# Q and K of one more token tile with tokens stationary, in a conditioned transformer block on one core

## The chip, the cores and the metric

The kernel runs on one core of one Trainium2 chip. The metric is the device time of one execution in microseconds, as the median of the runs shown. Engines are named as in the profile: PE (matrix products), DVE, ACT and POOL (vectors), SP (it issues nearly all transfers).

## The reference

One transformer block over 2048 tokens of 448 features, modulated by a vector `c`: dilated local attention (16 heads of 28, a window of 8 keys that are 2 tokens apart), then a GELU network of 1792 features. All in bfloat16.

```python
mod = (silu(c) @ w_mod).reshape(c.shape[0], 6, 1, -1)
sa, ca, ga, sb, cb, gb = ...
h = layernorm(x) * (1 + ca) + sa
# A: qkv = h @ wqkv; logits of token s against keys s, s-2, ..., s-14
#    attn = softmax(logits * 28 ** -0.5); o = attn @ v
x = x + ga * (o @ wo)
h = layernorm(x) * (1 + cb) + sb
# B: y = layernorm(h); gelu(y @ w1 + b1) @ w2 + b2
x = x + gb * B(h)
```

## The kernel before

**Tiles.** The tokens are dealt to two streams (even and odd), so that the dilated window becomes eight neighbouring tokens of one stream. Each stream has 1024 tokens, in 8 tiles of 128; a tile `p` of the code means 128 tokens of both streams. Attention goes in 9 batches of 114 queries of each stream.

**A tile's way.** `front_ln` takes the statistics (`stats`, `aggr`, `rstd`), normalizes into a buffer `zy` (`norm`, `tail`) and turns the features onto the partitions: tiles 0 and 1 by PE transposes (`tr0`, `tr1`), tiles 2 to 7 by DMA transposes on SP (`zT2` to `zT7`). The evacuation (`evac_h`, on ACT or DVE) applies scale and shift and writes `hT`. The scale and shift come from `mod_cols`, PE products of `w_mod` (buffers `wm_st`, `wm_r`, and `wm_d`, into which `twice` copies some columns on DVE), added up by `sca` on DVE.

**Q and K, in two ways.** `front_qk` keeps the weights stationary, which are first spread to 32 columns per head (`spread`, `spread r`); its result already has the features on the partitions, and one evacuation writes `qT` or `kT`. `natural_qk` keeps the tokens stationary (`hT` as weights, 448 columns of `wqk_st` moving): it needs no spread weights, but its result has the tokens on the partitions, so it is evacuated into a `zy` buffer and turned by a DMA transpose on SP (`tq`, `tk` with the tile's number, L631). The constant `NATURAL` says which tiles go the second way. Products of 64 rows (the last 64 of the 448 features) are issued apart from the full ones, as the `r` tasks beside the `f` tasks.

**Attention and the rest.** For batch i: V (`v`), scores (`lt`, two halves), exponential on ACT, mask on DVE, denominators (`pd`), weighted values (`po`), `omul` on DVE. Then for each tile `wo`, the first residual (`x1`), two layer norms and a DMA transpose (`yT`), and for two tiles at a time `w1`, GELU on ACT, `w2`, the last residual and the store. The products `mods` and a small round trip through memory give the other modulation rows.

**The order.** Nothing is scheduled at run time. The code records some 700 tasks with `add`, numbered in the order of recording, and `emit` issues them in the order of a list of numbers, `ORDER`; an entry `n:A`, `n:D`, `n:P` puts a task on ACT, DVE or POOL instead of its first engine, and `n:R` takes a V product with the rest first. An entry `n+18@m` issues 18 products of a zeroed tile (`filler`) ahead of task n, into the accumulator of task m. `SLOTS` gives each buffer its place; the products share four PSUM slots of two banks. Each engine runs its instructions in this order and waits where an operand or a slot isn't free. SP's transfers queue in its order too.

Of the kernel before, what the change touches and what calls it, by code (L numbers as in the profile page):

```python
# [14 lines left out]
S, D, H, DH, F = 2048, 448, 16, 28, 1792  # L15
# [17 lines left out]
EXP_SET = "natural_log_exp_and_others"  # L33
GELU_SET = "gelu_apprx_tanh_and_others"
UNITS = [[0], [1], [2, 3], [4, 5], [6, 7]]
NATURAL = range(2, 8)
PHASES = [(range(0, 5), [0]), (range(5, 7), [1]), (range(7, 9), [2, 3])]
ROOM = {"P": 4, "et": 2, "den": 2, "zy": 5, "h2": 3, "yT": 3, "hm": 2, "vb": 3, "xp": 3, "hw": 2}
SPLIT = 2
# [1 line left out]
ENGINE = {"A": "ACT", "D": "DVE", "P": "POOL", "R": "PE2"}  # L41
RATE = 310e3
SLOTS = [
# [6 lines left out]
]  # L50
ORDER = """
17 18 19 3 7 0 15 14 10 8 1 55+12@55 12 2 11 5 13 4 6 9 71 73 74 72 16 56 57 75 58 59 76 60 20 24 21 23 22 25 26 77 61
62 78 67 66 108 63+6@63 68 64 65 110 84:A 89:P 79 69 70 80 101 94 109 111 112:P 81 83 90 82 85:A 114 113 115:D 27 28
30 29 32 31 34 37 86:P 87 92:A 91:P 88:A 93:P 135 133 136 134 144 142 137 139 145 143 102 95 96 116 117:A 118:A 120:A
119:A 103 97 99 104 106 105 98 126 121 127 122 129 124 107 100 190 191 187 188 128 123 130 125 138 140:D 146 148 147
149:D 141 185 186 236:R 238 241 150 153:A 239 242 269 271 207 200 198 208 201 272 199 270 209 210 151 152 154 202 211
213 203 212 159 160 164 156 273 214 161 237 155 163 204 240 278 279 205:D 36 33 40 35 171 215 206 162 280 281 192 189
282:A 157 165 158 172 243 193 244 194 195 196 283 216 217 284 274 285:D 275 307:R 340 173 39 286 41 219 218 197 341:D
246 308 312 309 313 247 310 167 224 168 221 225 174 38 131 220 169 226 276:D 132 314 311 245 222 315 316 317 318 373
248 277 170 166 227 223 176 175 249 374 345 342 319 289:A 290:A 343 346 250 251 288:A 253 287 320 228 375 378 321  # L60
447:P 322 252 324 344 254 558:P 376 255 347 257 379 256 377 258 259 323 325 326 295 233 229 292 296 230 291 299 297
293 348 300 304 303 232 350 301 351 305 54 45 51 46 43 52 48 298 294 231 47 49 44 262 260 327 328 380 329 261 330 263
333 331 264 265 332 334 266 335 267 234 448 381 349 382 383 449 560 559 384 406 482:A 450 561 235 268 352 353 337 336
338 385 386 181 354 357 387 483 484 390 391 355 356 388 178 389 358 182 184 339 42 50 53 426 414 425 427 428 485 413
407 415 416 418 417 408 420 410 409 411 412 419 424 422 423 421 446 392 393 180 394 395 396 399 183 397 179 359 361
400 593:P 398 177 429 401 360 362 363 364 366 367 440 442 454 489 451 455 452 490 441 443 432 402 365 368 431 433 444
436 437 486 487 491 456 453 457 370 369 459 460 371:A 403 488 404 430 434 458 461 492 493 494 495 435 462 594 302 445
306 405 372 496 463 438 497 498 501 464 524 595 525 537 536 499 466 467 500 596:D 465 468 470 469 502 471 472 473 474
475 503 505 504 506 507 510 476 477 508 511 517 526 527 529 538 539 528 518 531 519 522 521 520 523 530 535 532 533
534 545 547 562 565 597 557 598 479 509 478 480:A 563 566 548 551 546 540 512 513 514 543 541 599 564 567 600 568 553  # L70
515:A 544 542 549 601 602 570 603 605 571 606 628 569 604 572 552 554 573 607 608 574 575 555 609 577 578 576 579 581
580 610 582 612 611 583 613 584 585 586 550 516 481 635 636 630 629 639 638 640 637 641 631 632 634 633 647 648 642
644 587 588 614 615 616 617 618 621 619 620 622 623 625 624 626:D 589 590 651 591 652 655 654 653 643 646 645 658 664
656 649 650 662 659 665 663 657 556 627 592 660 666 661 674 675 669 679 677 676 678 668 680 673 671 672 670 681 687
695 686 685 682 683 688 684 689 705 697 696 706 698 701 702 709 710 690 694 707 708 691 693 692 699 700 667 439 703
704 711 712
"""


# [74 lines left out]
def kernel(  # L154
# [18 lines left out]
    P = Plan()  # L173
# [336 lines left out]
    def front_ln(u, on_act, dma=False):  # L510
        np_ = len(u)
        if dma:
            zT = sb("yT", [128, NS * KT, 256], BF16, "zT")
        else:
            ptr = [psum("ptr", (128, np_, 2, NS, 128), BF16) for _ in range(2)]
        for q, p in enumerate(u):
            z = fixed("zy", zys)
            for n in range(NS):
                stats(lambda p=p, n=n: xn(p, n), 0, 2 * p + n, [f"x{p}"])
            rstd(0, 2 * p, 2, on_act)  # L520
            for n in range(NS):
                normalize(lambda z=z, n=n: z.t[:, n, 0:D], lambda p=p, n=n: xn(p, n), 0, 2 * p + n, [f"x{p}"],
                          bufs=[z], writes=[(z, n)])
            tail(z, [(z, 0), (z, 1)], (z, 2), p == 0)
            zk = [(z, 0), (z, 1), (z, 2)]
            if dma:
                add("SP", 2.0, lambda z=z, q=q: nc.sync.dma_start_transpose(
                    out=zT.t[:, :, 128 * q:128 * q + 128], in_=z.t[:].rearrange("p n e -> p (n e)")), reads=zk, bufs=[z, zT],
                    writes=[(zT, q)], xfer=1.0, name=f"zT{p}")
                continue  # L530

            def tr(q=q, z=z):
                for kt in range(KT):
                    for n in range(NS):
                        nc.tensor.transpose(out=ptr[kt % 2].t[:, q, kt // 2, n, :], in_=z.t[:, n, kt * 128:(kt + 1) * 128], identity=ident[:])
# [371 lines left out]
    for pi, (batches, tiles) in enumerate(PHASES):  # L907
# [55 lines left out]
```

## Time and profile before

| | |
|---|---|
| median of 3 runs | 171.34 us (170.38 to 173.87) |
| the profiled execution's own time | 169.54 us |
| its span, from the first to the last instruction | 167.7 us |
| PE, DVE, ACT, POOL busy | 96%, 69%, 63%, 27% of the span |
| mean granted TensorE clock | 0.999 |

The profile is of one execution. Busy shares are averages over the whole span; in a row of the timeline, the first number is the start in us from the span's start, the second the length, and the bracket at the end is the engine's idle time before it with what ended it. A `q` behind an engine's name is its queue, which issues transfers. Buffer numbers are left out of the names, and one line of code can stand for many tasks (L548 and L554 are the full and the 64-row products of every weight; L631 is every `tq` and `tk`).

### The profile page before, as it was taken

The numbers are of one execution on the slowest core, as the hardware profiler recorded it, in microseconds if no ns is written. First come the engines' busy times: TensorE is split into PE (matmuls) and PEld (weight loads), VectorE is DVE, ScalarE is ACT, GpSimd is POOL, SyncE is SP. The second block draws the span as 40 slices with busy tenths as digits, with TensorE's granted clock in tenths as the row PEclk, the third lists the DMA queues.
The fourth block names the chain that finished last, engine by engine and source line by source line (L and its number), as shares of the span: only waits on it lengthen the run. The fifth ranks groups of instructions, "written<-read, shape, count | busy, mean of one in ns | idle before, by whom it ended". The sixth has DMA issues, their size and how long they took to land.

```text
span 167.7 us, 4943 instructions
## 1 busy us (share of the span) xinstructions
PE 160.4 (96%) x2109; PEld 83.8 (50%) x2109; DVE 115.3 (69%) x268; ACT 105.2 (63%) x146; POOL 45.8 (27%) x72
## 2 busy tenths in 40 slices
PE   7779999999989999999999999999999999999993
PEld 4567655546444553445565444556534455444652
DVE  7798978937889989996567879893779650400032
ACT  3268799999878991869486086968428440086400
POOL 7063230000161301744340030850010347007200
PEclk9999999999999999999999999999999999999999
DMA  4998998999997998100075000009210005100024
GB/s 146 339 299 309 173 288 158 140 191 164 233 313 158 219 210 195 35 4 0 26 153 73 4 0 0 0 4 151 33 59 0 0 20 105 59 0 0 0 72 147
DMA packets 35573, 18.78 MB, mean 112 GB/s; under 512 B 28507, under 2 KB 34592, under 8 KB 35552
## 3 DMA queue, kind: packets, MB, share of 16 engines
q1 hardware_dynamic: 35548, 18.47, 48.7%
q8 instruction: 16, 0.26, 0.7%
q14 instruction: 5, 0.04, 0.1%
q10 hardware_dynamic: 4, 0.00, 0.0%
HBM read 9.81 MB, written 1.84 MB: 69 GB/s over the span
## 4 chain that ended last, share of the span: by engine, by line
PE 80%; DMA 7%; DVE 6%; ACT 4%; issue 1%; SPq 0%; DVEq 0%
PE p L883 26%; PE p L548 22%; PE pq L548 6%; PE pw L803 5%; PE p L554 4%; DMA kT<-zy 3%; PE po L771 3%; PE pv L548 3%; PE lt L738 2%; DMA b_rows<-in_B_b_dram 2%; DMA zT<-zy 2%; PE pq L562 2%; ACT et L745 2%; PE pq L554 2%; PE pd L760 1%; ACT vb L721 1%
## 5 line engine op out<-in xcount | busy, mean ns | idle before, releaser
L864 ACT ACTIVATE hm<-p,b_col 128x512 bf16<-128x512 f32 x56 | 33.9, 692 | 34.9 <-PE p L554 28.0
L883 PE MATMUL p<-w_s,hm 128*128 128x448 bf16 (+1 forms) x238 | 44.3, 342 | 0.0
L548 PE MATMUL p<-yT,w_s 128*128 128x512 bf16 x168 | 38.0, 379 | 0.0
L469 POOL TENSOR_TENSOR rs_all<-mvs,neg_half 128x2 f32<-128x2 f32 x22 | 16.4, 760 | 61.9 <-DVE mvs L458 61.8
L883 PEld LDWEIGHTS <-hm 128*128 128x128 bf16 x238 | 22.6, 98 | 19.5 <-issue 1.3
L889 DVE TENSOR_TENSOR x_all<-p,x1p 128x896 bf16<-128x896 f32 (+2 forms) x10 | 8.9, 900 | 26.6 <-PE p L883 26.6
L548 PEld LDWEIGHTS <-w_s 128*128 128x128 bf16 x168 | 16.0, 98 | 20.7 <-issue 2.5
L745 ACT ACTIVATE et<-lt 128x928 bf16<-128x928 f32 x18 | 16.2, 942 | 7.4 <-PE lt L738 7.3
L456 DVE BATCH_NORM_STATS2 stt<-x_all 128x6 f32<-128x448 bf16 x32 | 18.7, 612 | 0.3
L841 POOL TENSOR_TENSOR x1p<-x_all,gbb_bc 128x448 f32<-128x448 bf16 x16 | 17.2, 1099 | 0.0
L548 PE MATMUL pq<-wqk_st,hT 128*128 128x448 bf16 x72 | 15.0, 353 | 0.0
L788 DVE TENSOR_TENSOR qT<-po,den 128x912 bf16<-128x912 f32 x9 | 9.9, 1104 | 5.7 <-ACT den L782 4.9
L751 DVE TENSOR_TENSOR et<-et,mask 128x928 bf16<-128x928 bf16 x18 | 12.5, 724 | 1.7 <-ACT et L745 1.5
L803 PE MATMUL pw<-wo_s,qT 128*128 128x448 bf16 x64 | 13.1, 353 | 0.1
L819 DVE TENSOR_TENSOR h<-h,mod_bc 128x896 bf16<-128x896 bf16 x16 | 11.4, 710 | 0.3
L628 ACT CAST zy<-pq 128x896 bf16<-128x896 f32 x12 | 10.5, 907 | 0.5 <-issue 0.2
L810 DVE TENSOR_TENSOR x_all<-pw,x_all 128x896 bf16<-128x896 f32 x8 | 8.7, 1085 | 2.7 <-PE pw L803 2.7
L548 PEld LDWEIGHTS <-hT 128*128 128x128 bf16 x72 | 6.5, 98 | 6.4 <-issue 0.9
L782 ACT ACTIVATE den<-den,den_bias 128x928 f32<-128x928 f32 x9 | 9.5, 1066 | 0.2
L456 DVE BATCH_NORM_STATS2 stt<-h 128x6 f32<-128x448 bf16 x16 | 9.4, 611 | 0.2
L689 POOL COPY hw<-hT 128x1024 bf16<-128x1024 bf16 x3 | 3.3, 1114 | 22.7 <-ACT hT L504 22.7
L780 ACT ACTIVATE den<-pd 128x928 f32<-128x928 f32 x9 | 8.4, 939 | 1.1 <-PE pd L760 1.1
(114 smaller groups left out, 183.4 us busy)
## 6 DMA issues: line engine op xcount, KB each, us to landing
w_s<-in_B_w_dram SPq DMA_DIRECT2D x7, 224.0 KB, 3.4
out_dram<-x_all SPq DMA_DIRECT2D x7, 224.0 KB, 2.2
x_all<-in_A_x_dram SPq DMA_DIRECT2D x3, 448.0 KB, 4.6
wmod<-in_w_mod_dram SPq DMA_DIRECT2D x3, 448.0 KB
w_s<-in_B_w_dram SPq DMA_DIRECT2D x3, 448.0 KB, 4.7
wqk_st<-in_A_wqkv_dram SPq DMA_DIRECT2D x3, 225.0 KB
wm_st<-in_w_mod_dram SPq DMA_DIRECT2D x1, 672.0 KB
x_all<-in_A_x_dram SPq DMA_DIRECT2D x2, 224.0 KB
```

Of the source, the lines that this page charges most:

```text
L456: add("DVE", 0.53, lambda: nc.vector.bn_stats(out=stt[:, w, b, 0:6], in_=src()), reads=reads, bufs=bufs, after=early if w == b == 0 else ( ...
L469: ways = {"POOL": (0.55 + 0.17 * n, lambda: nc.gpsimd.tensor_tensor(out=r, in0=v, in1=neg_half[:, 0:n], op=ALU.pow))}
L548: nc.tensor.matmul(out(), lhsT=lhs(kt, slice(0, 128)), rhs=rhs(kt, slice(0, 128)), start=first and kt == 0, stop=not first and kt == KT - 2)
L554: nc.tensor.matmul(out(), lhsT=lhs(KT - 1, rows), rhs=rhs(KT - 1, rows), start=first, stop=not first, tile_position=(rows.start, 0))
L628: add("ACT", 0.80, lambda to=to, src=src: nc.scalar.copy(out=to(), in_=src()), bufs=[pq, st], reads=["zpad"], writes=[(st, 0)], name="evac ...
L745: exps.append(add("ACT", 0.83, lambda half=half, lt=lt: nc.scalar.activation(out=et.t[:, 2 * half:2 * half + 2].rearrange("p r m c -> p r ...
L751: nc.vector.tensor_tensor(out=ev, in0=ev, in1=mask[:], op=ALU.mult)
L803: nc.tensor.matmul(pw.t[:, s, 0:D], lhsT=qT[:, KT * s + ft, LEAD + 128 * p:LEAD + 128 * p + 128], rhs=wo_s[:, ft, :], start=(ft == 0), sto ...
L819: add("DVE", 0.55, lambda vec=vec, op=op: nc.vector.tensor_tensor(out=h2.t[:], in0=h2.t[:], in1=vec.unsqueeze(1).to_broadcast([128, NS, D] ...
L841: add("POOL", 1.0, lambda n=n: nc.gpsimd.tensor_tensor(out=x1p.t[:, n, :], in0=xn(p, n), in1=gbb2_bc[:], op=ALU.add), reads=[f"x{p}", "gbb ...
L864: gelus.append(add("ACT", 0.585, lambda f=f, a=a, p1=p1s[g]: nc.scalar.activation(out=hm.t[:, f].rearrange("p n c -> p (n c)"), in_=p1.t[: ...
L883: nc.tensor.matmul(p2.t[:, n, 0:c1 - c0], lhsT=hm.t[:, f, n, q * 128:(q + 1) * 128], rhs=w2_s[:, f, c0:c1], start=(f == parts[0][0]), stop ...
```

## The change

`NATURAL` now begins at tile 1, so tile 1's Q and K go through `natural_qk`: 12 full products of 448 columns and 4 of 64 rows, two evacuations into `zy` buffers and two DMA transposes (`tq1`, `tk1`), in place of 24 full products of 256 columns, 8 of 64 rows, and two evacuations straight into `kT` and `qT`. Tile 0 keeps `front_qk` and its spread weights. As the tasks' numbers shift, `ORDER` and `SLOTS` are replaced as a whole, and they are other orders throughout, not the old ones with one insertion.

```diff
-NATURAL = range(2, 8)
+NATURAL = range(1, 8)
...
-    0, 0, 1, 1, 0, 0, 0, 0, 1, 2, 3, 0, 0, 1, 2, 3, 0, 2, 3, 0, 0, 1, 0, 2, 3, 1, 2, 0, 4, 3, 0, 3, 0, 0, 0, 1, 0,
+    0, 0, 1, 1, 0, 0, 0, 0, 1, 2, 3, 0, 1, 2, 0, 3, 1, 0, 3, 3, 2, 1, 0, 0, 1, 1, 0, 0, 3, 2, 1, 2, 2, 2, 1, 1, 0,
...
-62 78 67 66 108 63+6@63 68 64 65 110 84:A 89:P 79 69 70 80 101 94 109 111 112:P 81 83 90 82 85:A 114 113 115:D 27 28
+68+18@68 108 110 109 111 76 63 64 112 4 67 69 78 65 113 70 114 89:A 84:P 79 80 94 22 25 29 31 30 28 32 35 38 83 81 86
...
     for k, u in enumerate(UNITS[0:2]):
         front_ln(u, True)
-        if k == 0:
+        if k == 0 and u[0] not in NATURAL:
             spread(0)
             spread(1)
         if u[0] in NATURAL:
             natural_qk(u[0])
```

What the lists move, at the places that the prediction speaks of:

On PE, the zero products ahead of the first `mod_cols` become 18 from 6, and they write the accumulator of the second one (task 68 in the line above), not of the first (task 63), whose slot `c_cols` used. The scores of batch 1 come behind the Q of tiles 2 and 3 and two more products of tile 2, no longer ahead of them.

On DVE, at the start of the program, where `zy_96` is tile 0's normalized rows and `wm_d` the copied columns of `w_mod`:

```order
-L478 TENSOR_SCALAR zy_96<-x_all,mvs,rs_all 128x448 x2
-L418 COPY wm_d<-wm_st 128x6x64 x2
+L418 COPY wm_d<-wm_st 128x6x64
+L418 COPY wm_d<-wm_r 128x64
+L418 COPY wm_d<-wm_st 128x6x64
+L478 TENSOR_SCALAR zy_96<-x_all,mvs,rs_all 128x448
+L456 BN_STATS stt<-x_all 128x6 x2
+L458 BN_AGGR mvs<-stt 128x2 x2
+L478 TENSOR_SCALAR zy_96<-x_all,mvs,rs_all 128x448
```

Both halves of tile 0's norm stood ahead of the copies; now the copies stand ahead of them, and the statistics of tile 1 between the halves.

On SP, behind the loads of the input, where `zT` is the transposed norm of tiles 2 and 3 first and then of tiles 4 and 5, and `wmod` the weights of `mods`; first before, then after:

```order
L527 DMA_TRANSPOSE zT<-zy_97 128x8x128
L527 DMA_TRANSPOSE zT<-zy_96 128x8x128
L362 DMA wmod_283<-in_w_mod_dram 64x1792
L362 DMA wmod_283<-in_w_mod_dram 128x1792
L366 DMA wo_s<-in_A_wo_dram 28x4x448
```

```order
L527 DMA_TRANSPOSE zT<-zy_96 128x8x128
L527 DMA_TRANSPOSE zT<-zy_97 128x8x128
L631 DMA_TRANSPOSE qT<-zy_98 128x8x128
L362 DMA wmod_280<-in_w_mod_dram 64x1792
L362 DMA wmod_280<-in_w_mod_dram 128x1792 x2
L631 DMA_TRANSPOSE kT<-zy_99 128x8x128
L527 DMA_TRANSPOSE zT<-zy_100 128x8x128
```

The two transposes of tile 1 stand around the weights of `mods`, ahead of the transposes of tiles 5 and 4.

On SP some twenty rows later, up to the transposes of tile 4's Q and K, for which the scores of batch 4 wait; first before (the last four rows are `tq3`, `tk3`, `tq4`, `tk4`), then after (`tq3`, `zT6`, `zT7`, `tk3`, `tk4`, `tq4`):

```order
L650 DMA mod_bc<-mod_hbm 128x1792
L366 DMA wo_s<-in_A_wo_dram 28x4x448
L527 DMA_TRANSPOSE zT<-zy_97 128x8x128
L631 DMA_TRANSPOSE qT<-zy_96 128x8x128
L631 DMA_TRANSPOSE kT<-zy_100 128x8x128
L631 DMA_TRANSPOSE qT<-zy_99 128x8x128
L631 DMA_TRANSPOSE kT<-zy_98 128x8x128
```

```order
L650 DMA mod_bc<-mod_hbm 128x1792
L631 DMA_TRANSPOSE qT<-zy_98 128x8x128
L527 DMA_TRANSPOSE zT<-zy_99 128x8x128
L527 DMA_TRANSPOSE zT<-zy_96 128x8x128
L631 DMA_TRANSPOSE kT<-zy_97 128x8x128
L631 DMA_TRANSPOSE kT<-zy_98 128x8x128
L631 DMA_TRANSPOSE qT<-zy_100 128x8x128
```

Tile 4's Q goes out behind its K, and tile 6 is transposed behind `tq3` and no longer ahead of all four.

More of the change, by code (lines that the diff above doesn't have):

```diff
@@ L56 @@
[L56 to L75, printed above, removed]
@@ L76 @@
-704 711 712
+0 1 11 17 18 15 14 16 3 10 6 55+12@55 56 5 9 2 13 12 71 19 20 24 21 23 27 26 57 72 73 58 74 75:P 59 61 66 62 77 60
+68+18@68 108 110 109 111 76 63 64 112 4 67 69 78 65 113 70 114 89:A 84:P 79 80 94 22 25 29 31 30 28 32 35 38 83 81 86
+115 91:P 90 82 85:A 93:P 88:A 87:P 133 131 134 132 142 140 135 136 141 137 138 143 92:A 116 101 102 103 119:A 118:A
+120:A 117:A 95 96 97 99 104 106 105 98 144:A 207 146 145 208 147 122 126 125 121 107 127 198 196 205 267 278 199 206
+276 277 197 7 200 8 100 123 209:A 211 234 139 148 128 36 34 33 183:R 185 188 279 150 152 149 235 151:A 186 201 268 210
@@ new lines @@
+202 203:A 184 189 166 165 212 187 167:D 269 190 124 157 153 154 158 270 155:D 159:D 213 204 37 191 193 169 192 156 236
+239 170 194 237 240 160 305 338:R 171 306 216 214:A 215 238 241 271 217 195 273 280 281 445:P 242 244 339 40 39 161
+307 310 172 162 223 272 274:D 282 283 163:D 308 311 309 312 245 222 224:D 218 313 243 314 168 275 174 173 246 315 316
+317 284 219 227 226 164 220 247 228 221 225 318 340 343 287:A 285:A 341 344 248 288 286 251 249 319 252 250 446 447
+373 376 377 374 448 50 44 229 46 45 54 591:P 253 320 322 255 254 345 378 256 323 257 375 321 260 342 480:P 324 258 261
@@ L77 @@
+259 326 325 262 327 264 328 263 331 332 293 297 298 231 294 302 230 295 299 301 232 347 379 346 303 371 348 381 349
+372 382 329 330 265:D 289 481 380 350 482 290 593 296 43 53 48 47 51 333 334 335 336:D 592 41 266 383 384 594:D 385
[7 rows of a table added]
+604 626 510 539 475 477 476 540 478 511 543 545 546 544 512 513:D 570 571 605 606 572 607 608 547 609 575 576 610 611
[5 rows of a table added]
 """
```

3 lines of the change are left out of this document (removed), and 22 rows, old and new, of tables (ORDER, SLOTS).

## The prediction

> **What bounds the kernel now.** I read the page's first two parts, then the chain that ended last in order of time, then the timeline of the first 48 us.
>
> ```profile
> span 167.7 us, 4943 instructions
> PE 160.4 (96%) x2109; PEld 83.8 (50%) x2109; DVE 115.3 (69%) x268; ACT 105.2 (63%) x146; POOL 45.8 (27%) x72
> PE   7779999999989999999999999999999999999993
> GB/s 146 339 299 309 173 288 158 140 191 164 233 313 158 219 210 195 35 4 0 26 153 73 4 0 0 0 4 151 33 59 0 0 20 105 59 0 0 0 72 147
> ```
>
> TensorE is busy in every slice from the fourth to the last but one. So a product that leaves PE is worth its own length, and a wait is worth something only where PE stands in it. The chain in order of time shows where that is:
>
> ```profile
> 41.71 4.87 DMA kT<-zy
> 46.63 0.70 PE lt L738 x62
> ...
> 63.82 0.32 issue
> 64.13 0.82 PE p L554 x6
> ```
>
> Past the start the chain is PE with two visible holes: the transpose of a K tile that lands for the scores of batch 4, and 0.32 us ahead of the first `w1` product. The end (a last product, an addition, a store) is the same code after the change.
>
> **Part 1: the products of tile 1.** Timeline of the program before, PE:
>
> ```profile
> 14.07 2.79 PE L548 MATMUL pq<-hT,Wqk 128*128 128x256 bf16 x24
> 16.80 0.61 PE L554 MATMUL pq<-hT,Wqr 64*128 64x256 bf16 x8
> 17.97 1.48 PE L548 MATMUL pq<-hT,Wqk 128*128 128x256 bf16 x12
> ...
> 24.28 0.82 PE L554 MATMUL pq<-wqr_st,hT 64*128 64x448 bf16 x6
> ...
> 33.12 2.44 PE L548 MATMUL pq<-wqk_st,hT 128*128 128x448 bf16 x12
> ```
>
> Ends of products are modelled, so a row runs a little into the next (14.07 + 2.79 against the start at 16.80); I take 0.07 us off each. With the weights stationary, tile 1 costs 24 full products (twice the dozen, 2 x 1.41) and eight of 64 rows (0.54): 3.3 to 3.4 us. With tokens stationary it costs 12 full products of 448 columns (2.37) and four of 64 rows (two thirds of 0.75): 2.9. **-0.4 us**, all on PE and so on the path. On ACT two evacuations of 1024 columns become two of 896, which saves 0.2 us off the path.
>
> **Part 2: the start of PE's work.** Timeline of the program before:
>
> ```profile
> 1.26 2.74 PE L382 MATMUL ps_c<-warm_w 128*128 128x256 bf16 x12 [1.26 <-DVE warm_w L242]
> 5.52 1.44 PE L382 MATMUL ps_col<-warm_w 128*128 128x256 bf16 x6 [0.99 <-DVE silu_bf L396]
> 5.53 0.70 DVE L478 TENSOR_SCALAR zy<-x_all,mvs,rs_all 128x448 bf16<-128x448 bf16 x2
> 6.92 0.43 DVE L418 COPY wm_d<-wm_st 128x384 bf16<-128x384 bf16 x2 [0.69 <-DMA wm_st<-in_w_mod_dram]
> 7.38 0.27 DVE L418 COPY wm_d<-wm_r 128x64 bf16<-128x64 bf16 x2
> 7.92 1.01 PE L535 MATMUL ptr<-ident,zy 128*128 128x128 bf16 x8
> 9.19 0.25 DVE L458 BATCH_NORM_AGGREGATE mvs<-stt 128x2 f32<-128x9 f32 x2
> 9.31 1.02 ACT L504 ACTIVATE hT<-ptr,mod_col 128x256 bf16<-128x256 bf16 x2
> 9.93 2.29 PE L562 MATMUL pq<-hT,Wqk 128*128 128x256 bf16 x10 [0.86 <-ACT hT L504]
> 10.23 0.61 ACT L441 COPY Wqk<-wqk_st 128x512 bf16<-128x512 bf16 x1
> 10.73 0.83 ACT L449 COPY Wqr<-wqr_st 64x256 bf16<-64x256 bf16 x2
> 12.01 1.06 PE L535 MATMUL ptr<-ident,zy 128*128 128x128 bf16 x8
> 12.04 1.15 DVE L456 BATCH_NORM_STATS2 stt<-x_all 128x6 f32<-128x448 bf16 x2
> 12.90 1.93 ACT L504 ACTIVATE hT<-ptr,mod_col 128x256 bf16<-128x256 bf16 x4 [1.33 <-PE ptr L535]
> ```
>
> Two things move, against each other. **Later:** before, tile 0 is normalized while `wm_st` is still on its way. Now the copies that need `wm_st` stand ahead of it on DVE, and the statistics of tile 1 between its halves. From 6.92: three copies 0.57, a norm 0.35, two statistics 1.15, two aggregates 0.25, a norm 0.35, and some 0.4 for two small memsets, the last copy and the tail: the transposes of tile 0 start at 10.0 and not at 7.92. Then come the two `sca` and a norm of tile 1 (to 10.7) and ACT's evacuation (0.5): Q/K of tile 0 starts at **11.2 and not at 9.93**. **Faster:** before, ten products take 2.08 us from 9.93 to 12.01, 0.21 us each; in the row of 24 quoted above, the same form takes 0.114 each. The quick rate sets in after some 3.5 us of unbroken work. Now 18 zero products follow `c_cols` with no wait for `silu` (their accumulator's slot is another), so PE is busy from 1.26 to 7 or 8, which is longer than the stretch that brought the quick rate before. If the rate lasts through the thin stretch to 11.2, twelve products save 1.2 us and the transposes of tile 1 0.4: 12 x 0.11 + 0.4 + 0.6 + 1.4 us of work put the end of tile 0's Q/K at 15.0.
>
> What then holds is tile 1's `hT`, by ACT's order: 10.7, two evacuations 1.0, a spread 0.6, two rest spreads 0.8, four evacuations 1.9: 15.1. The spread needs weight slice 1, which is now loaded behind 560 KB more; at the 300 GB/s of the page's third and fourth slices that is 1.9 us, some time before 12, and about when ACT comes to it. So tile 1's Q/K starts at 15.1. Before it started at 14.07 + 12 x 0.114 = 15.4. **-0.3 us**, between -0.4 (PE's own 15.0) and **+1.2**: with the slow rate from 11.2, the same work ends at about 16.6, since the quick rate comes back only after 3.5 us.
>
> The row of the ten products is where a rule speaks against the change. The Trainium skill, "TensorE: Matmul & The Clock Gate", section "What's actually happening", has the array at half rate until a window of about 3.4 us was busy, and again after an idle one. The 0.21 and 0.114 us agree with its two rates; before, the array had never been busy for a whole window ahead of 9.93. Between 8.3 and 11.2 the changed kernel gives it only the transposes of tile 0 and two small products: by the rule, a wholly idle window does not fit in, so the quick rate stays, and if nearly idle counts as idle the sum is 1.5 us higher.
>
> **Part 3: the wait for tiles 2 and 3.** Timeline of the program before:
>
> ```profile
> 15.57 3.10 SPq L527 DMA_TRANSPOSE zT<-zy  x2
> 19.39 3.08 PE L706 MATMUL pv<-Wv,hT 128*64 128x448 bf16 x32
> 20.61 1.06 DVE L502 TENSOR_SCALAR hT<-zT,mod_col 128x512 bf16<-128x512 bf16 x3 [0.16 <-DMA zT<-zy]
> 22.10 0.85 ACT L504 ACTIVATE hT<-zT,mod_col 128x512 bf16<-128x512 bf16 x1
> 23.04 1.31 PE L548 MATMUL pq<-wqk_st,hT 128*128 128x448 bf16 x6
> ```
>
> Their `hT` is complete at 22.95, and PE takes it at 23.04 without standing still, because the scores of batch 1 stood ahead of it. The change sets these scores (0.7 us) behind. PE then has from 15.1: tile 1 2.9, `v1` and `v0` 3.0, the scores of batch 0 0.6: it is there at 21.6. DVE's sequence (evacuations and spreads of tiles 0 and 1 to 12.3, four statistics 2.3, their aggregates, two norms, the tail on POOL) brings the first transpose to about 15.9 (before 15.57), the landing of the second to about 20.7 and the last evacuation to about 22.0. **+0.4 us** of idle PE, between 0 and 1.
>
> **Part 4: two more transposes in the queue.** All transposes go out on SP, in order; the answer for their line, the timeline's row of batch 4's scores, and the stage before it:
>
> ```profile
> L631 SPq DMA_TRANSPOSE qT<-zy x6: 1232/1275/2026, 26.7 to 83.2; - x6
> DMA to landing us min/median/max: 4.4/4.8/5.1
> ...
> 46.63 0.70 PE L738 MATMUL lt<-qT,kT 28*64 28x58 bf16 x64 [0.79 <-DMA kT<-zy]
> ...
> 40.00:44.00 4.00, 3.90 (x86) 1.93 (x83) 3.28 (x5) 3.83 (x6) 0.00 (x0) 1.00 1.22 154
> ```
>
> Each holds SP for 1.3 us (the median) and lands 4.8 us after its issue began, and the DMA engines are full there (the stage's row prints a share of 1.22). The change adds `tq1` and `tk1`: 2.6 us of SP, between `zT3` and `zT5`. Queued behind `tq1` are the three loads for `mods`, behind `tk1` the transposes of tiles 5 and 4, and behind all of them those that batch 4's scores need. In the program before, SP issues the last of these at 41.71. In the changed order `tk4` and then `tq4` end that row. I follow PE from tiles 2 and 3 at 22.0: the same products, batch for batch, as before stand ahead of tile 4's K, whose product ends, by the lengths of the rows, near 39; ACT evacuates it by about 40.6, `tk4` begins then, `tq4` at 41.9, and lands at 46.7. PE comes to those scores after one tile's V and two `wo` tiles, at about 45.6. A hole of 1.1 us, against 0.8: **+0.3 us**. Bounds: none at all (-0.8) where PE comes later, and 0.8 + 2.6 = 3.4 us (**+2.6**) if all that the two transposes take arrives here.
>
> **Part 5: what else moved.** Four PSUM slots serve everything, so a product may wait for the evacuation of the product before it in its slot. The new order gives DVE five evacuations of Q/K that ACT had; DVE has that room, with 69% busy. I find no new wait over 0.3 us on the way from 22 to 39, and the small ones of before go: **0**, between -0.5 and +1.0. Ahead of `w1`, the wait of 0.32 hangs on `yT1`, which DVE brings; as many DVE operations stand between the first `x1` and it as before: **0**, between -0.3 and +1. From there on PE has the same products, one V tile exchanged for another, in a stretch without a hole: **0**.
>
> **The sum**, against the profiled execution, whose own time is 169.5 us (its span 167.7 and 1.8 around it): -0.4 - 0.3 + 0.4 + 0.3 = 0.0. That execution is 1% below the median of 171.3, so I carry the sum over as a difference: 171.3 us. The bounds add up to -2.4 and +5 or so if all fall one way, which they don't do together, as a PE that comes late at one place finds the next transpose landed.
>
> **The rivals.**
> - *The queue decides.* The two added transposes delay every later one, and the hole at batch 4's scores grows by up to 2.6 us. For it: the share of 1.22, and that 0.8 us are lost there already. Against it: the stages around 40 have short breaks in the queue, and PE reaches the place with other work first. It decides once `tq4` is issued after 42.5, and gives 172.5 to 174.5, **slower**: 20%.
> - *The quick rate is lost by 11.2* (part 2). For it: a thin stretch of 3 us such as the program before has nowhere once PE is at work. Against it: 0.8 us of idle at 45.8 does not slow it. It gives 1.5 more, 172.8: 10%.
> - *The holes close.* -0.4 and -0.3 stay, `hT` of tiles 2 and 3 is in time, the scores of batch 4 find their tiles, `yT1` is there for `w1`: -0.4 - 0.4 - 0.8 - 0.3 = -1.9, or 169.4, and with the lower bound of part 5 168.9. For it: PE's own products have to be done, and nothing else has; against it: three independent chains must all be better. 22%.
> - The forecast, waits that move but weigh about the same, 170.3 to 172.3: 48%.
>
> A difference of under 2% (3.4 us) is about what a measurement of this kernel can't tell from none; its three runs spread as widely. Faster than 167.9 would take all of the lower bounds and a little more: 6%. Slower than 174.8 takes the queue's full price and another: 10%. Within 2%: 84%. The range goes from 168.9, the closed holes, to 174.0, most of the queue's rival.
>
> **What the profile after would show.** Part 1: no weight-stationary product of 256 columns past tile 0, and two more groups of 448 columns in their place. Part 2: the first product of tile 0 near 11.2, at 0.11 us from one to the next, and 18 zero products right behind `c_cols`; 0.21 would show the rate lost. Part 3: an idle PE near 21.6 with `zT` as its releaser. Part 4: a wait of the scores of batch 4 for `kT` or `qT` of about 1 us, and no long wait elsewhere for a transpose. What would make the forecast wrong is a wait in the stretch from 64 us on, which I take to be as dense as before, or a load (weight slice 1, the `mods` weights) that lands later than by its bytes.

## The result, and the profile after

The changed kernel takes 175.65 us (174.76 to 178.08) against 170.86 us before on the same chip, 1.0275 times as long (95% interval 1.02 to 1.0349): **slower**, where 171.3 and no measurable difference were forecast. A second set of runs (e10 below) gave 175.27 us and 1.0277 (1.0219 to 1.0335). Ratios here are of undisturbed (fast) runs alone, against such runs of the kernel before on the same chip. The profiled execution took 175.6 us, with a span of 173.6 us.

Page of the changed kernel, the parts that answer to those shown of before, the row of the granted clock (tenths of full speed in 40 slices) and the share of the DMA engines:

```profile
span 173.6 us, 4946 instructions
PE 161.9 (93%) x2105; PEld 82.8 (48%) x2105; DVE 117.2 (68%) x270; ACT 101.3 (58%) x141; POOL 44.5 (26%) x76
PE   7749999798999999999959999999999999999993
PEclk9975999999999999999999999999999999999999
DMA  5999689979999997930025000001700017110002
```

PE is no longer dense: slice 3 (8.7 to 13.0 us) has fallen to 4, slice 21 (86.8 to 91.1) to 5, and the clock shows 7 and 5 in slices 3 and 4. The first thin place in the timeline of PE:

```profile
9.24 0.19 PE L410 MATMUL ps_col<-silu_bc,wm_d 64*128 64x32 bf16 x2 [1.50 <-DVE wm_d L418]
10.52 0.38 PE L562 MATMUL pq<-hT,Wqk 128*128 128x256 bf16 x2 [0.54 <-POOL zy L490]
13.37 1.89 PE L562 MATMUL pq<-hT,Wqk 128*128 128x256 bf16 x8 [1.47 <-DVE Wqk L439]
16.16 2.32 PE L548 MATMUL pq<-hT,Wqk 128*128 128x256 bf16 x12
18.41 0.55 PE L554 MATMUL pq<-wqr_st,hT 64*128 64x448 bf16 x4
```

Tile 0's Q/K starts at 10.52, then stands 1.47 us for the spread of weight slice 1. Its last 12 products take 2.25 us (18.41 - 16.16), 0.19 each and not 0.11. Tile 1's Q/K starts at 18.41, where it was 15.44 before (14.07 and 12 times 0.114). The slice is late because its load is. Here are waits from 5 to 14.5 us (us in total, times, longest), and SP's row for the load:

```profile
ACT Wqk L441 <- DMA wqk_st<-in_A_wqkv_dram: 2.1, 1, 2.1
DVE Wqk L439 <- DMA wqk_st<-in_A_wqkv_dram: 1.8, 1, 1.8
6.41 0.33 SPq L325 DMA_DIRECT2D wqk_st<-in_A_wqkv_dram  x1
```

ACT stands 2.1 us and starts its spread at 13.02; the load went out at 6.41 (before, all three slices were out at 4.99) behind the extra 560 KB. The second thin place, in the timelines of SP, DVE and PE:

```profile
69.46 1.33 SPq L631 DMA_TRANSPOSE kT<-zy  x1
70.83 1.12 SPq L375 DMA_DIRECT2D w_s<-in_B_w_dram  x2
73.79 1.16 DVE L661 TENSOR_TENSOR w_s<-w_s,mod_bc 128x896 bf16<-128x896 bf16 x2 [2.61 <-DMA w_s<-in_B_w_dram]
90.08 0.37 PE L760 MATMUL pd<-et,ones_k 64*32 64x464 bf16 x2 [1.81 <-DVE et L751]
```

Two parts of the second MLP weight go out behind a transpose at 70.83, 3.1 us after the first `w1` product (67.70); before, SP issued the last of them at 62.81, ahead of that product:

```profile
62.81 0.94 SPq L375 DMA_DIRECT2D w_s<-in_B_w_dram  x2
```

DVE has to scale each part, stands 2.61 us for them, and everything queued behind on DVE comes later, the masks of batch 5 among it: PE waits 1.81 us for these masks at 88.3.

Three marks in the timeline of PE (the first three columns) cut the span into a start, a middle and phase 2, which begins with the first `w1` product. The last column is the mean clock of the profiled execution; runs e1 to e14 are told below.

| kernel | tile 1's Q/K starts | first `w1` product | PE ends | middle | phase 2 | clock |
|---|---|---|---|---|---|---|
| before | 15.44 | 64.13 | 164.77 | 48.7 | 100.6 | 0.999 |
| changed | 18.41 | 67.70 | 170.75 | 49.3 | 103.1 | 0.980 |
| changed, again (e10) | 15.23 | 65.68 | 170.21 | 50.5 | 104.5 | 0.99 |
| e1, slice first | 13.95 | 64.31 | 166.94 | 50.4 | 102.6 | 0.998 |
| e3, w2 early | 15.20 | 66.20 | 167.32 | 51.0 | 101.1 | 0.999 |
| e5, both | 15.13 | 65.86 | 166.99 | 50.7 | 101.1 | 1.0 |
| e9, both, tile 1 as before | 13.91 | 63.37 | 164.48 | 49.5 | 101.1 | 1.0 |
| e12, e9 with two idle transposes | 13.99 | 65.48 | 166.59 | 51.5 | 101.1 | 1.0 |
| e13, e9 with six small loads | 13.95 | 63.56 | 164.66 | 49.6 | 101.1 | 0.998 |

The 6.0 us by which PE ends later in the first profile are 3.0 at the start, 0.6 in the middle and 2.4 in phase 2. The same kernel in e10 ends 5.4 us later, of which -0.2, 1.8 and 3.9: where the time is lost differs from one execution to the next.

### The profile page after: what moved, and what is told of

Its sections match the earlier page's. It is cut to its first block, busy times and chain, and to the rows that moved or that the text cites. A ratio compares the mean times of both kernels' runs of the same rounds, so it can differ in the third digit from the quotient of the medians.

```text
span 173.6 us, 4946 instructions
## 1 busy us (share of the span) xinstructions
PE 161.9 (93%) x2105; PEld 82.8 (48%) x2105; DVE 117.2 (68%) x270; ACT 101.3 (58%) x141; POOL 44.5 (26%) x76
## 5 line engine op out<-in xcount | busy, mean ns | idle before, releaser
L469 POOL TENSOR_TENSOR rs_all<-mvs,neg_half 128x2 f32<-128x2 f32 x21 | 14.9, 712 | 57.0 <-DVE mvs L458 53.7
L548 PE MATMUL pq<-wqk_st,hT 128*128 128x448 bf16 x84 | 17.3, 353 | 0.0
L751 DVE TENSOR_TENSOR et<-et,mask 128x928 bf16<-128x928 bf16 x18 | 11.1, 634 | 3.4 <-ACT et L745 3.2
L548 PEld LDWEIGHTS <-hT 128*128 128x128 bf16 x84 | 7.6, 98 | 8.3 <-issue 2.1
L819 DVE TENSOR_TENSOR h<-h,mod_bc 128x896 bf16<-128x896 bf16 x16 | 10.5, 661 | 0.3
L628 ACT CAST zy<-pq 128x896 bf16<-128x896 f32 x9 | 8.0, 910 | 3.9 <-PE pq L548 2.1
L478 DVE TENSOR_SCALAR h<-x_all,mvs,rs_all 128x448 bf16<-128x448 bf16 x16 | 8.8, 581 | 1.8 <-POOL rs_all L469 1.6
```

Source lines behind the costliest of these rows:

```text
L469: ways = {"POOL": (0.55 + 0.17 * n, lambda: nc.gpsimd.tensor_tensor(out=r, in0=v, in1=neg_half[:, 0:n], op=ALU.pow))}
L548: nc.tensor.matmul(out(), lhsT=lhs(kt, slice(0, 128)), rhs=rhs(kt, slice(0, 128)), start=first and kt == 0, stop=not first and kt == KT - 2)
L751: nc.vector.tensor_tensor(out=ev, in0=ev, in1=mask[:], op=ALU.mult)
L819: add("DVE", 0.55, lambda vec=vec, op=op: nc.vector.tensor_tensor(out=h2.t[:], in0=h2.t[:], in1=vec.unsqueeze(1).to_broadcast([128, NS, D] ...
```

## The experiments

e1 to e4 change one thing of the changed kernel each. In kernels whose lists are a line shorter, line numbers are lower by one (by eight where `SLOTS` stands on one line).

**e1: weight slice 1 and its last rows loaded first.** (22, 26, 25: the loads of the slice and the rows; 27: x of tiles 2 to 7)

```diff
-... 24 21 23 27 26 57 ... 80 94 22 25 29 ...
+... 24 21 23 22 26 25 27 57 ... 80 94 29 ...
```

> The changed kernel with weight slice 1 of Q/K and the two 64-row pieces loaded ahead of x of tiles 2 and 3 again, as before the change; nothing else moved. Theory 'start': PE's 1.5 us wait for the spread of that slice at 11.9 to 13.4 goes, tile 1's hT is ready near 14.5 and its Q/K starts at 15.0 to 16 (18.4 in the changed kernel); the end moves with it by 2 to 3 us, span 170.5 to 171.5. Rival 'later stages hold': x of tiles 2 and 3 lands 1.5 us later, their transposes with it, and what the start gains is waited away before 30 us: span within 0.7 of 173.6.

173.56 us, 1.0246 (1.0206 to 1.0285). By the ratios the gain is 0.3%, within the error, so what follows rests on the stages of one execution, the fastest of the four (171.82 us). No product waits for the slice, the clock is full from 5.1, tile 1's Q/K starts at 13.95, earlier than the 15.0 to 16 that were expected. Timeline of PE:

```profile
13.95 0.55 PE L553 MATMUL pq<-wqr_st,hT 64*128 64x448 bf16 x4
21.61 0.36 PE L553 MATMUL pq<-wqr_st,hT 64*128 64x448 bf16 x2 [1.08 <-DVE hT L501]
86.27 0.37 PE L759 MATMUL pd<-et,ones_k 64*32 64x464 bf16 x2 [1.43 <-DVE et L750]
```

Part of the gain goes at 20.5, where PE now waits for `hT` of tiles 2 and 3; the stall of phase 2 is untouched. The start is one loss, and not the only one.

**e2: PE kept busy at the start.** (711: 13 zero products behind the first small ones; 16 more ahead of Q/K)

```diff
-... 63 64 112 ... 116 101 102 ...
+... 63 64 711 112 ... 116 101+16@101 102 ...
```

> The changed kernel with 13 more zero products between the third and the last group of mod_cols, and 16 ahead of the second product group of tile 0, where PE had idled; loads and order otherwise the same. Theory 'rate': the granted clock does not fall at 11.1 us, the products of tile 0 from 13.4 on take 0.11 us and not 0.21, tile 1's Q/K starts at about 16.4 (when its hT is complete) and not 18.4, the end moves by 1.5 to 2: span 171.5 to 172. Rival 'window': the clock falls anyway, or the later stages take the gain: span within 0.7 of 173.6.

175.75 us, 1.033 (1.0257 to 1.0404): no gain. The rate holds at the start, and tile 1's Q/K begins at 15.93. But PE then stands 1.40 us at 38.9, and the clock is halved from 41.90 to 45.31. So the rate that was kept at the start was lost behind a later wait.

**e3: the second MLP weight earlier.** (52, 49: two of its loads; 266: `yT0`)

```diff
-... 592 41 266 383 ... 300 52 49 292 ...
+... 592 41 52 49 266 383 ... 300 292 ...
```

> The changed kernel with the two last w2 loads issued by SP ahead of the first yT transpose (SP idles there, 59.6 to 61.6) and no longer behind the transposes of tile 7; nothing else moved. Theory 'late w2': DVE's 2.6 us wait for that load at 71 to 74 goes, the masks of batches 5 and 6 come in time, PE's wait of 1.8 us for the mask at 88 to 90 goes, the end moves by 1.5 to 2.2: span 171.4 to 172.1. Rival 'DVE full': the masks are late because DVE has more work there than before, the wait stays: span within 0.5 of 173.6.

172.5 us, 1.0179 (1.0145 to 1.0214). Phase 2 falls from 103.1 to 101.1, and the wait of 1.81 is gone from PE's timeline:

```profile
86.66 0.37 PE L759 MATMUL pd<-et,ones_k 64*32 64x464 bf16 x2
87.20 0.38 PE L759 MATMUL pd<-et,ones_k 64*32 64x464 bf16 x6 [0.17 <-DVE et L750]
```

The load is what makes the masks late. In this execution the clock stayed full at the start, though the code up to there is the changed kernel's; tile 1's Q/K started at 15.20. Weight slice 1 also came earlier: its spread starts at 11.85, where the changed kernel's starts at 13.02. So the 18.41 of the changed kernel is this 15.2 with a slice that came 1.2 us later and the rate lost.

**e4: the weights of `mods` ahead of `tq1` in SP's queue.** (36, 34, 33: these loads; 128: `tq1`)

```diff
-... 139 148 128 36 34 33 183:R ...
+... 139 148 36 34 33 128 183:R ...
```

> The changed kernel with the three loads for mods issued ahead of tq1 (SP idles 19.6 to 21.2) and no longer between tq1 and tk1; nothing else moved. Theory 'queue': tk1 lands earlier by about 2 us, the waits of batch 1's scores (0.45 for kT, 0.6 for a buffer that tk1 still reads) go, the stage to 44 us ends about 1 us earlier: span 172.5 to 173. Rival 'absorbed': the waits come back at the next place in the queue or are hidden by the late start of the stage after: span within 0.4 of 173.6.

178.11 us, 1.0491 (1.0418 to 1.0564): worse than everything else. PE stands 3.34 us behind the first denominators of batch 0, for a mask of DVE, and the clock is halved for two windows after it:

```profile
30.37 0.38 PE L759 MATMUL pd<-et,ones_k 64*32 64x464 bf16 x6 [3.34 <-DVE et L750]
```

Timeline of DVE:

```profile
28.15 1.09 DVE L628 CAST zy<-pq 128x896 bf16<-128x896 f32 x1 [4.00 <-DMA qT<-zy]
```

DVE stands 4.00 us, by the profile until `tq1` has read the `zy` buffer that this evacuation writes, and the mask stands behind it in DVE's order. The only transpose into `qT` issued by then is `tq1`, which now goes out at 20.74 behind the three loads (at 19.18 in e10). So neither theory held: moving the loads ahead only moved the wait to `tq1`.

**e5: both moves, of e1 and of e3.**

> The changed kernel with both moves of the first two trials that helped: the loads of weight slice 1 and of its last rows ahead of x of tiles 2 to 7 (e1), and the loads of the second MLP weight ahead of the transpose yT0 (e3). Theory (two separate losses, start and phase 2): the lengths add up. Start as in e1 (Q/K of tile 1 at 13.9 to 14.1, clock full at the start), from the first W1 product to the end 101.1 as in e3 and not 102.6 as in e1, the wait at the fifth score sums (1.43 in e1) gone; span 168 to 168.5, time 170 to 172 by how often the rate falls. Rival (the loads share the queues): the earlier second MLP weight lands on top of the k and q transposes of batches 3 and 4 and the middle grows by what phase 2 gives: 173 to 174.

171.92 us, 1.0085 (1.0046 to 1.0125). By the ratios the two misplaced loads together are worth 1.9% of the 2.8% (each move alone gave 0.3 and 1.0, with errors of some 0.8). The clock is part of it: its mean stands at 0.99 in two of the ten runs, and at 0.971 to 0.99 in nine of the changed kernel's ten. Phase 2 came as expected. The start did not: 15.13 and not about 14, as the first load of `w_mod` was late in this execution (DVE's first copy at 7.05, 5.80 in e1). What is left against the kernel before sits mostly in the middle, 50.7 us against 48.7.

**e6: tile 1 by weights stationary, the rest as changed.**

```diff
-NATURAL = range(1, 8)
+NATURAL = range(2, 8)
-... 122 126 125 121 ... 127 ... 123 ... 128 ... 124 ...
+... 126 121 127 122 129 124 128 123 ... 125 ... 130 ...
```

> The changed kernel with tile 1's Q and K by weights stationary as before (NATURAL from 2), everything else, loads, extra zero products, order and slots, as changed; its two transposes and two zy buffers go. Theory A (tile 1's turned Q/K is what lengthens the middle: the transposes in SP's queue, the zy buffers and the wait of batch 1's scores): from Q/K of tile 1 to the first W1 product 48.7 or less where the changed kernel has 49.3 (50.4 in e1, where the rate stays): the waits of lt1 (0.45 and 0.63) go; the start and phase 2 stay as they are, so span 171.5 to 173, time 173.5 to 175. Theory B (the new order of the other steps costs the middle): the middle stays at 49.5 to 51 and the time at 175.5 to 176.5, with 0.4 more for the products.

172.95 us, 1.0148 (1.0061 to 1.0235). The time speaks for theory A (by the ratios it gained 1.3%, 2.2 us), the stage for B (50.3 from tile 1's Q/K, with 0.4 of products more). Phase 2 fell as well, to 101.7: with two transposes fewer, SP reaches the last of the late loads at 67.5 to 68.2, not at 70.8 to 71.5. This run alone does not decide; e9, held beside e5, does.

**e7: tile 1 turned in the order of before**, with the scores of batch 1 behind tile 2's first Q/K.

```diff
-... 126 121 127 122 129 124 ... 190 ...
+... 122 126 125 121 ... 188 ...
-... 238 241 150 153:A ...
+... 148 124 128 151:A ... 157 158 236 239 ...
```

> The kernel before with only tile 1's Q and K turned by DMA: the transposes tk1 and tq1 stand behind zT3 on SP, the two zy buffers in slots 3 and 4, and the scores of batch 1 with their exponentials are put behind the first Q/K of tile 2, since kT of tile 1 is there only then. Theory A: the stage grows by the waits that the transposes bring, 1 to 2 us for batch 1's scores, less 0.4 of products: 171 to 172.5. Theory B: tile 1's turned Q/K costs nothing by itself, 169.5 to 170.5. Both expect the start as before (clock full from 13.7, tile 1's Q/K at 15.4) and phase 2 as before (100.6).

175.58 us, 1.0276 (1.0167 to 1.0385): as slow as the whole change, and beyond what either theory expected. Waits of PE from 14 to 70 us:

```profile
PE lt L730 <- DMA kT<-zy: 1.7, 2, 1.2
PE pq L546 <- ACT et L737: 1.3, 2, 0.8
PE p L546 <- DMA yT<-zy: 1.0, 1, 1.0
PE pv L698 <- ACT zy L620: 0.8, 1, 0.8
PE pv L698 <- ACT et L737: 0.8, 1, 0.8
PE lt L730 <- DMA qT<-zy: 0.7, 1, 0.7
```

Phase 2 is as before (100.6); the middle is 54.7, with waits for transposes and for evacuations behind them. With only these steps moved, the order of before does not carry the turned tile; a better order around it was not tried.

**e8: before, with 18 zero products into the free slot.**

```diff
-... 108 63+6@63 68 ...
+... 108 63+18@68 68 ...
```

> The kernel before with 18 zero products into the free slot (as the changed kernel has them) in place of the 6 that wait for silu; nothing else. Theory (the quick rate at the start is worth its time where the loads stand as before): the products of tile 0's Q/K go at 0.11 from 9.93 on, so tile 1's Q/K starts 1.3 us earlier than 15.44, and if that is passed on the time is 169.4 to 170. Rival (hidden): the turned zT2 and zT3 hold Q/K of tile 2 at the same time as before, 23.0, or the windows of the clock fall so that a wait of 1 us at 8.9 takes the rate away: 170.3 to 171.5.

171.65 us, 1.0096 (1.004 to 1.0153). Q/K of tile 0 runs at the quick rate and tile 1's starts 0.9 us earlier, but:

```profile
33.05 0.44 PE L737 MATMUL lt<-qT,kT 28*64 28x58 bf16 x32 [1.03 <-DVE qT L787]
64.19 0.82 PE L553 MATMUL p<-yT,w_r 64*128 64x512 bf16 x6 [0.21 <-issue]
```

The scores of batch 2 wait for their PSUM slot, and `w1` starts when it did before (64.13). The rival holds: the earlier start was worth nothing there, and by the ratio the kernel is 1.0% slower.

**e9: e5 with tile 1 as before** (the edits of e1, e3 and e6 together).

> The changed kernel with the two moves of loads of e5 (weight slice 1 and its last rows ahead of x of tiles 2 to 7; the second MLP weight ahead of yT0) and with tile 1's Q and K by weights stationary as before, its two transposes gone. To be held beside e5, which differs only in tile 1's Q/K. Theory B (the new order of the other steps costs the middle, tile 1's turned Q/K next to nothing): from Q/K of tile 1 to the first W1 product 50 to 51 as in e5 (50.7) and e6 (50.3), phase 2 101.1, time 171.5 to 172.5. Theory A (tile 1's transposes cost the middle what the runs still lack): middle 48.7 to 49.5, time 170 to 171.

169.79 us, 0.9971 (0.9933 to 1.0009). Theory A: the middle is 49.5 us, as the theory put it, and by the ratios tile 1's turned Q/K costs 1.1%, 1.9 us with an error of about 0.9, with all else equal (e5). The two profiled executions differ by 2.5 us, but 1.2 of that lies ahead of tile 1's Q/K, where both have the same order and e5's first load of `w_mod` was late (DVE's first copy at 7.05, here at 5.88). The other 1.3 lie in the middle. This is the best version run: 3% under the changed kernel, not to be told from the one before. B falls.

**e10: the changed kernel again.**

> The changed kernel itself, once more, beside e9 and e11 on one chip, to see in how many runs the granted clock of the whole span stands below 0.995, and by how much these are longer. Theory (a wait of 1.5 us at 7.7 and at 11.9 takes the rate for one or two windows of 3.4 us in most runs): 0.97 to 0.99 in at least 7 of 10 runs, and runs with a full clock at 172.5 to 173.5, as e3 less its gain of phase 2 turned round. Rival (the four runs so far were chance): most runs at 0.999 and the median at 173.

175.27 us, 1.0277. In five of six runs the mean clock was 0.99, at 174.7 to 176.2 us; the one with a full clock took 173.73, a little above what was expected. The rival falls. The profiled one kept its rate at the start and lost it in phase 2. Windows of that execution (PE's busy time is the first number behind the comma, the clock is the 1.00 or 0.50):

```profile
83.15:86.56 3.41, 3.06 (x46) 1.48 (x39) 3.38 (x10) 0.94 (x1) 0.15 (x1) 1.00 0.00 0
86.56:89.97 3.41, 1.84 (x136) 1.44 (x137) 3.05 (x6) 0.94 (x1) 1.09 (x3) 1.00 0.40 77
89.97:93.39 3.42, 3.42 (x21) 1.31 (x16) 1.49 (x2) 3.36 (x4) 0.00 (x0) 0.50 0.64 81
```

The stall at 86.2 (1.74 us) costs its own length, and then a window of 3.4 us at half rate, 1.7 us more: phase 2 took 104.5. At the start, weight slice 1 came earlier than in the first profile (ACT's row, then PE's):

```profile
11.88 0.62 ACT L441 COPY Wqk<-wqk_st 128x512 bf16<-128x512 bf16 x1 [1.41 <-DMA wqk_st<-in_A_wqkv_dram]
12.24 1.05 PE L562 MATMUL pq<-hT,Wqk 128*128 128x256 bf16 x8 [1.12 <-DVE Wqk L439]
15.23 0.56 PE L554 MATMUL pq<-wqr_st,hT 64*128 64x448 bf16 x4
```

**e11: e8 with the PSUM slot freed** (three entries of `SLOTS`: the scores' first half to slot 3, Q of tile 3 to 0, the `b1` row to 3).

> A version meant to beat both: the kernel before with 18 zero products into the free slot (e8, which starts 1.0 us earlier and loses it at 32.0, where the scores of batch 2 wait 1.03 for batch 1's weighted values to leave their PSUM slot) and with that slot given to the next Q/K instead: scores of batch 2, first half, to slot 3, Q of tile 3 to slot 0, the b1 row to slot 3. Theory (the slot is what holds it): the wait at 32.0 goes to 0.1 or less, the first W1 product starts 0.7 to 1.0 earlier than 64.2, time 168.8 to 169.6 in undisturbed runs, ratio 0.993 to 0.998. Rival (the exponentials of ACT, busy from 25 to 35, hold the batch anyway): the wait moves to the sums of batch 2 at 38 and W1 starts at 64.2, ratio 1.00 to 1.01.

171.1 us, 1.0026 (0.9987 to 1.0065). A miss: the wait of 1.05 us moved from the scores to the product that took the slot, and `w1` started at 64.93. This exchange of slots found no slack there.

**e12: e9 with two transposes that nobody waits for.** (713 and 714, where `tq1` and `tk1` stand in e5)

```diff
+    scr = cst.tile([128, 8, 128], BF16, name="scr")
+    def turn(i):
+        add("SP", 1.25, lambda: nc.sync.dma_start_transpose(out=scr[:], in_=Wqk[:, i].rearrange("p a h e -> p (a h e)")), ...)
```

> e9 (new order, both loads moved, tile 1's Q/K as before) with two more transposes of 128x1024 that nobody waits for: from Wqk into a tile that is never read, where tq1 and tk1 stand in SP's queue in e5 (behind zT3, and behind the three loads of the mods' weights, ahead of zT5). Theory D (SP's queue and the DMA engines' time: two transposes more, SP held 1.3 us by each, push what stands behind them): the stage from Q/K of tile 1 to the first W1 product grows from 49.4 to 50.5 or more, and the time from 169.8 to 171 to 172, next to e5's 171.9. Theory W (who waits for tile 1's kT, qT and the two zy buffers): nothing waits for these two, so the stage stays at 49.4 and the time at 169.6 to 170.2.

171.34 us, 1.0046 (1.0011 to 1.0081). Theory D: the middle grows from 49.5 to 51.5 us, and by the ratios the time by 0.75%, 1.3 us. So two transposes that no instruction waits for cost most of what tile 1's cost. SP's timeline of e9, then of e12:

```profile
17.94 1.69 SPq L354 DMA_DIRECT2D wmod<-in_w_mod_dram  x3
24.05 2.61 SPq L519 DMA_TRANSPOSE zT<-zy  x2
```

```profile
18.30 1.28 SPq L928 DMA_TRANSPOSE scr<-Wqk  x1
19.63 1.69 SPq L354 DMA_DIRECT2D wmod<-in_w_mod_dram  x3
21.47 1.24 SPq L928 DMA_TRANSPOSE scr<-Wqk  x1
24.13 4.08 SPq L519 DMA_TRANSPOSE zT<-zy  x2
```

SP is free again at 22.71 and issues `zT5` at 24.13, where e9 issues it at 24.05. So up to there SP's queue was not late. But the pair now holds SP for 4.08 us instead of 2.61, and what stands behind it goes out later.

**e13: six small loads in the place of these two.**

> e9 with six loads of 64 numbers each (of c into a tile that is never read), three where tq1 and three where tk1 stood: they hold SP like the two transposes of e12 (some 0.45 to 0.6 us each by the small loads of the traces, 1.3 to 1.8 per place) and move next to nothing. It splits theory D. D1 (SP's time: what stands behind in its queue is issued later): the stage from Q/K of tile 1 to the first W1 product grows to 50.5 to 51.5 as in e12 (51.4), time 170.8 to 171.6. D2 (the DMA engines' time: 0.52 MB more in packets of under 512 B, in a stretch where their share stands at 1.0): the stage stays near 49.4 and the time at 169.6 to 170.2.

170.82 us, 1.0037 (1.0 to 1.0073). The loads held SP for 1.01 and 0.87 us, less than intended. The stage stands with D2: the middle is 49.6, but in an execution of 169.69 us, the second fastest of twelve. The times stand with D1: the median lies in the range that D1 gave, and the ratio is 0.7% (1.1 us) above e9's and 0.1% below e12's. So the split between SP's time and the DMA engines' time stays open.

**e14: Q and K of tiles 2 and 3 by weights stationary, too.** (`NATURAL = range(4, 8)`, four transposes fewer, K's second part behind the scores of batch 1)

> The other way: e9 with Q and K of tiles 2 and 3, too, by weights stationary (NATURAL from 4), four transposes and four zy buffers fewer; K's second part stands behind the scores of batch 1, and V of batch 3 ahead of V of batch 2. Products cost PE 0.8 more (24 full of 512 columns and 8 of 64 rows for the two tiles, against 24 of 448 and 8 half as dense). Theory D (a turned tile costs the queue and the DMA engines more than it saves PE, as long as they are full): the waits of the middle, some 2 us in e9, shrink by more than 0.8, time 168.5 to 169.6, ratio under 0.995. Rival (with the two transposes of tile 1 gone the queue no longer decides, and the new products and their evacuations, all needed at once by the scores of batch 2, cost their own length): 170.3 to 171.5.

175.89 us, 1.0366 (1.0306 to 1.0426). The rival, and worse than it. Timeline of PE:

```profile
29.54 0.77 PE L763 MATMUL po<-et,vb 64*32 64x57 bf16 x64 [1.15 <-DVE qT L602]
38.24 0.44 PE L730 MATMUL lt<-qT,kT 28*64 28x58 bf16 x32 [1.86 <-ACT den L772]
```

New waits on evacuations and on ACT take more than the four transposes gave back. As the rest of the order was made for other steps, this run does not price the four transposes.

## Why the prediction was wrong, point by point

**Part 1 (products, -0.4): right.** 12 products of 448 columns in 2.37 us (18.90 to 21.27) and four of 64 rows in 0.49: 2.86 us; e9 spends 3.32 on the same tile (12.54 to 17.23, less tile 0's 1.37).

**Part 2 (start, -0.3): wrong, +3.0 in the first profile.** Two terms failed in that execution. Weight slice 1 was put "some time before 12" by its bytes; its spread began at 13.02, 1.1 us later than in e10 (11.88), where the order is the same and the slice did come as forecast. From there to tile 1's Q/K the first profile takes 5.04 us (13.37 to 18.41) and e10 2.99 (12.24 to 15.23): the other 2.1 us are the quick rate, which was lost. I had argued that only a wholly idle window takes it away.

Where the rate held (e3, e10), tile 1's Q/K starts at 15.2, and 15.1 was forecast. That this fits is partly luck. Tile 0's transposes start at 8.9 in e10 and not at 10.0, as `wm_st` was there at 5.80 and not at 6.92, and ACT then stands 1.41 us for the slice; with the slice loaded first (e1) tile 1's Q/K starts at 13.95.

Windows of the changed kernel, in the 3.41 us steps in which its clock changes:

```profile
4.25:7.66 3.41, 3.31 (x51) 2.59 (x49) 2.19 (x11) 0.47 (x2) 0.70 (x1) 1.00 0.99 322
7.66:11.08 3.42, 1.38 (x23) 1.13 (x20) 3.42 (x16) 1.94 (x5) 1.46 (x3) 1.00 1.04 281
11.08:14.49 3.41, 1.94 (x13) 1.15 (x11) 1.60 (x6) 1.42 (x4) 0.79 (x2) 0.50 1.08 286
14.49:17.91 3.42, 3.42 (x21) 1.90 (x20) 3.41 (x12) 2.48 (x7) 1.15 (x3) 0.50 0.77 267
```

PE was busy for 1.38 of 3.42 us in the window ahead of the drop, and it stayed at half rate until a whole window had been dense. In e10 the windows lie 0.4 us later in the span, PE was busy for 1.79 of 3.42 us in the thin one (8.05 to 11.47), and the rate stayed. The rule of the Trainium skill weighed in part 2 ("TensorE: Matmul & The Clock Gate", section "What's actually happening") has the window of 3.4 us right, and its free-running start; its "idle" does not cover a window that was busy for 0.40. I gave this outcome 10% and 1.5 us; it took 2.1 here.

**Part 3 (hT of tiles 2 and 3, +0.4): right in kind.** In e10, where the start ran as forecast, PE waits 0.6 us there; in the first profile PE came so late that nothing was left to wait for.

**Part 4 (two transposes, +0.3): the term was mis-sized.** The turned tile costs 1.9 us by the ratios of e5 and e9 (with an error of about 0.9), and 1.3 by their middles; with the 0.46 of products that it saves, its transposes and the waits they bring cost 1.7 to 2.3. By e12 two idle ones cost 1.3 us in the times and 2.0 in the stage. It lies within the bounds I kept (up to +2.6), and is near the rival to which I gave 20%. The place was wrong too: the scores of batch 4, at which I put the hole, start at 50.35 without a wait, and the delay shows in small ones, here at the scores of batch 1 (the last row is batch 4):

```profile
31.56 0.56 PE L738 MATMUL lt<-qT,kT 28*64 28x58 bf16 x32 [0.45 <-DMA kT<-zy]
32.76 0.42 PE L738 MATMUL lt<-qT,kT 28*64 28x58 bf16 x29 [0.63 <-DVE zy L629]
50.35 0.46 PE L738 MATMUL lt<-qT,kT 28*64 28x58 bf16 x35
```

In e10 the longest wait of the middle is that of the `mods` products for their weights:

```profile
28.43 1.05 PE L641 MATMUL pb<-wmod,silu_bc 128*32 128x448 bf16 x16 [1.28 <-DMA wmod<-in_w_mod_dram]
```

These loads stand between `tq1` and `tk1` and go out at 20.53; in e9 they go out at 17.94, and PE does not wait for them. I had named them as a load that might land late, and put the wait at nothing. What the rest of the price consists of stays open: e12's SP rows and the stage of e13 speak for the DMA engines, whose row on the page stands at 6 to 9 tenths or more in every slice from the second to the sixteenth (69 us), and e13's times for SP's own time.

**Part 5 (from 64 us on, 0): wrong, +2.4.** I had named a wait from 64 us on and a load later than by its bytes as what would make the forecast wrong, and did not follow the second MLP weight's loads in SP's queue, though the order showed them. The step that failed is this overlap, put at nothing: the masks of batch 5 stand on DVE behind the scaling of that weight, and PE stood 1.81 us for them. e3 takes 1.9 of the 2.4 away; of the remaining 0.5, 0.2 is a wait in the denominators, and the rest was not traced. In e10 the same stall also cost the rate, and phase 2 was 3.9 us longer than before.

**The sum.** By the ratios the 2.8% are 1.9 for the two places of loads with the clock that they cost (e5), 1.1 for the turned tile (e9), and -0.3, within its error, for everything else. The upper bounds of the parts add up to +6.4 us, and not to "+5 or so"; the measured +4.8 lies inside them. I had set the range narrower, to 174.0, because I took it that they don't come together, and here the start or its rate, the transposes and phase 2 did.

## What to carry to other kernels

Follow each load in the new queue order up to the instruction that needs it, in every phase: here two loads behind a few hundred KB or behind a transpose cost 1.9%, the step that was changed 1.1%. Price a transpose that is added to a busy queue even where nobody waits for it: two such cost 1.3 us here, more than the 0.46 us of products that turning a tile saved. Count a PE wait of 1.4 us or more as a risk to the matrix clock too: in e10 a wait of 1.74 us was followed by 1.7 us lost to the half rate, while in e1 a wait of 1.43 us at the same place was not. And compare stages in more than one execution before a stage's loss is given a cause.

## What the runs showed of the hardware

- **The clock falls after a partly busy window.** Drops were seen behind windows of 3.41 us in which PE was busy for 0.13 (e4), 0.40 (changed), 0.54 (e10) and 0.59 (e2) of the time, and behind none above 0.60. It is no fixed threshold: windows with 0.48 to 0.57 passed without one (e1, e2, e4, e6, e10, e14). The same start lost the rate in one execution of the changed kernel and kept it in e10, where the windows lie 0.4 us later in the span and the thin one was busy for 0.52.
- **Two transposes that nobody waits for cost time.** They add 0.52 MB in e12 and cost 1.3 us by the ratios, 2.0 in the stage. At the 300 GB/s of the first slices' loads their bytes would take 1.7 us, as an estimate, so no more than their bytes is needed to explain it. The Trainium skill, "DMA: Bandwidth & Descriptors", section "Latency and other measured facts", gives DMA transposes 261 GB/s where a middle dimension is not contiguous; as an estimate by that page, 0.52 MB take 2.0 us. The stage of e12 agrees with that and the times (1.3) lie below it; no run here shows whether the page's condition holds for these transposes.
- **The issue of a transpose can hold SP far longer than usual.** A pair held SP for 2.61 us in e9 and 4.08 in e12, though it began at the same time (24.05 and 24.13). It is not only full engines that hold it: from 26.10 to 26.80 us of e12, in the middle of that hold, they moved 8 GB/s.
